# Attention and gated FFN on one core: q laid out as 128 partitions by 4 with 64 queries apart

## The chip, the core and the metric

The program runs on one core of a Trainium2 chip. The metric is the device time of one execution in microseconds (us), the median of several. Engines are called PE (TensorE, matmuls; PEld is its weight load), DVE (VectorE), ACT (ScalarE), POOL (GpSimd) and SP (SyncE, which here only issues DMAs). SP and ACT issue hardware DMAs, POOL issues software DMAs; all run on the same 16 DMA engines.

## The reference

For 8 batches and 8 heads, q, k and v are 1152 x 64 in fp32. Neighbouring pairs of q rows are averaged (so 576 queries), then softmax attention with scale 1/8, then the heads are laid side by side (x is 4608 x 512), and a feed-forward part without a nonlinearity follows:

```python
q_pool = q.reshape(B, H, S // 2, 2, D).mean(axis=3)
scores = scale * np.matmul(q_pool, k.transpose(0, 1, 3, 2))
attn = np.exp(scores - max); attn = attn / (sum + 1e-09)
x = matmul(attn, v).transpose(0, 2, 1, 3).reshape(B * S, H * D)   # 4608 x 512
a = x @ w1; b = x @ w2                                           # 512 -> 1024
out = ((a * b) @ w3) @ w_out                                     # 1024 -> 1024 -> 512
```

## The kernel before

**Pairs.** Two heads of one batch make a pair; there are 32 pairs (8 batches by 4). For each pair the kernel loads k, q and v into `kst`, `qst` and `vst` (lines 178, 180, 186; 576 KB each), casts k to fp16 (`kpair`, line 192), adds neighbouring q rows into fp16 (`qs`, line 198; on DVE for pair 0, on POOL for the others) and casts v with an extra column for the row sum (`vaug`, line 205). `qst` has 96 partitions (QP) with 6 pooled queries each (QC), for each head 3072 contiguous bytes a partition. Query 6p + c stands in partition p, block c, so after a transpose the columns of `qpT` hold the queries in the order c, p: a permutation that the output store undoes.

**Transposes.** Scores need d on the partitions. For pairs 0 to 7 PE transposes (`transp_pe`, lines 221 and 224: six blocks of q, nine of k, into one PSUM tile, then three DVE copies at lines 225 to 227). For pairs 8 to 31 SP issues DMA transposes (`transp`, lines 210 and 212), one pair ahead of their use.

**Scores and values.** `scores` (line 240) walks the 9 x 576 columns of a pair in groups of 512 into PSUM tiles `psc` (three of them), and ACT writes the exponentials into an SBUF ring (line 245). `av_pair` (line 259) multiplies 128 queries at a time ("unit": five per pair, the fifth overlaps the fourth and only its last 64 rows are new) with `vaug` into `avb`, and `av_norm` (lines 276, 284) divides by the row sum.

**xT.** The FFN needs x transposed: `xT` has 4 slots of 128 feature rows (one per pair of a batch) by 2880 columns, a ring of five batches of 576 columns. Units of pairs 0 to 19 get there by a PE transpose (line 289) and a DVE copy (line 296), those of pairs 20 to 31 by two DMA transposes per pair on SP (lines 269 and 271: 4 blocks of 128 and one of 64 columns).

**FFN.** w3 @ w_out is folded into `T16` early (lines 315, 324). The 4608 columns of `xT` are worked off in 9 chunks of 512: 16 groups of 4 matmuls (line 345, two per hidden block, evacuated at 365 or 367 and multiplied at 370), then 4 output tiles of 128 rows (line 377), scaled into `osb` (three buffers; lines 383, 386, 387, 390) and stored (line 355). The very last tile of chunk 8 is computed in two halves (lines 399, 401) and stored from ACT's queue. Because a 128-row tile crosses the 96-row blocks of the query order, `store` cuts each tile into two DMAs.

**Order.** It is written out by the Python code, not by a scheduler: in each visit three groups of scores, one or two units of `av_pair`, and one or two groups of the FFN queue ("fill"). A chunk joins the queue when the unit that completes it is done (`done_at`); chunks that depend on DMA-transposed x wait ten units more (`held`). After the last scores come the rest of the units and then the rest of the queue, chunks 6 to 8, with ACT helping to evacuate (`tail`).

**Queues.** Loads of pairs 0 and 1: SP and ACT. Loads of pairs 2 to 9: POOL, with w3, w_out, w1 and w2 between them. Loads from pair 10 on (v from pair 8 on) and all DMA transposes: SP, in program order. Output stores before the tail: POOL; in the tail: SP. At the end all engines read a flag (line 583), and SP waits for every DMA to land.

Of the kernel before, what the change touches and what calls it, by code (L numbers as in the profile page):

```python
# [8 lines left out]
FP32 = mybir.dt.float32  # L9
FP16 = mybir.dt.float16  # L10
AF = mybir.ActivationFunctionType
ALU = mybir.AluOpType
# [11 lines left out]
def _general(tc, q, k, v, out, w1sb, w2sb, T16):  # L24
# [8 lines left out]
    NF = dff // 128  # L33
    QP = 96
    QC = Sq // QP
    SCALE = 0.5 * float(D) ** -0.5
# [3 lines left out]
    with tc.tile_pool(name="gen", bufs=1) as sb, \  # L40
# [3 lines left out]
        for h in range(H):  # L44
# [5 lines left out]
            nc.sync.dma_start(out=vst, in_=vf[bass.ds(ih, 1)].rearrange("o (c p) d -> p (o c) d", p=128))  # L50
            qst = sb.tile([QP, QC, 2, D], FP32, tag="g_qst")
            nc.sync.dma_start(out=qst, in_=qf[bass.ds(ih, 1)].rearrange("o (c p t) d -> p (o c) t d", p=QP, t=2))
            kh = sb.tile([128, NJ, 128], FP16, tag="g_kh")
            qh = sb.tile([QP, QC, 128], FP16, tag="g_qh")
            vh = sb.tile([128, NJ, D], FP16, tag="g_vh")
# [6 lines left out]
            nc.sync.dma_start(out=kT, in_=kh.rearrange("p c d -> p (c d)"), transpose=True)  # L62
            qT = sb.tile([128, QC, QP], FP16, tag="g_qT")
            nc.sync.dma_start(out=qT, in_=qh.rearrange("p c d -> p (c d)"), transpose=True)
            kTf = kT.rearrange("p c i -> p (c i)")
            pav = ps.tile([128, 1024], FP32, tag="g_pav")
            for c in range(QC):
                pss = ps.tile([128, S // W, 512], FP32, tag="g_pss")
# [24 lines left out]
        for ft in range(NF):  # L93
            for n0 in (0, NH):
# [8 lines left out]
                nc.vector.tensor_tensor(out=gT[:, ft, n0:n0 + NH], in0=pb[:, 0:NH], in1=asb, op=ALU.mult)  # L103
        for c in range(QC):
            po = ps.tile([128, 512], FP32, tag="g_po")
# [9 lines left out]
def kernel(  # L115
# [11 lines left out]
    nc = tc.nc  # L127

    B, H, S, D = q.shape
    Sq = S // 2  # L130
# [5 lines left out]
    HP = H // 2  # L136
# [2 lines left out]
    G = 512  # L139
    NS = NP * FLAT // G  # L140
    RING = 24 * Sq
    QP = 96
    QC = Sq // QP
    E1 = D + 1
    SCALE = 0.5 * float(D) ** -0.5
    SCL = 16.0
    TO = [0, 128, 256, 384, Sq - 128]
    NT5 = len(TO)
# [6 lines left out]
    att = fast.enter_context(tc.tile_pool(name="att", bufs=2))  # L155
# [3 lines left out]
    ident16 = const.tile([128, 128], FP16)  # L159
# [13 lines left out]
    kq, vs, pairs = {}, {}, {}  # L173

    def load_kq(p, k_eng, q_eng):
        b, h0 = p // HP, 2 * (p % HP)
        kst = att.tile([128, 2, NJ * D], FP32, tag="kst")
        k_eng.dma_start(out=kst, in_=k[b, h0:h0 + 2].rearrange("u (p c) d -> p u (c d)", p=128))
        qst = att.tile([QP, 2, QC * 2 * D], FP32, tag="qst")
        q_eng.dma_start(out=qst, in_=q[b, h0:h0 + 2].rearrange("u (p c) d -> p u (c d)", p=QP))  # L180
        kq[p] = (kst, qst)

    def load_v(p, eng):
        b, h0 = p // HP, 2 * (p % HP)
# [2 lines left out]
        vs[p] = vst  # L187

    def cast_kq(p):
        kst, qst = kq.pop(p)  # L190
        kpair = att.tile([128, NJ, 2, D], FP16, tag="kpair")
        nc.gpsimd.tensor_copy(out=kpair.rearrange("p c u d -> p u c d"),  # L192
                              in_=kst.rearrange("p u (c d) -> p u c d", d=D))
        qs = att.tile([QP, QC, 2, D], FP16, tag="qs")
        qv = qst.rearrange("p u (c t d) -> p u c t d", t=2, d=D)
        eng = nc.vector if p == 0 else nc.gpsimd
        for u in range(2):
            eng.tensor_tensor(out=qs[:, :, u, :], in0=qv[:, u, :, 0, :], in1=qv[:, u, :, 1, :], op=ALU.add)  # L198
        pairs[p] = [kpair, qs]

    def cast_v(p):
        va = vaugs[p % NVA]
# [2 lines left out]
        nc.gpsimd.tensor_copy(out=va[:, :, :, 0:D], in_=vs.pop(p).rearrange("p u (c d) -> p u c d", d=D))  # L205

    def transp(p):
        kpair, qs = pairs[p]
        kT2 = att.tile([128, NJ, 128], FP16, tag="kT2", bufs=3)
        nc.sync.dma_start(out=kT2, in_=kpair.rearrange("p c u d -> p (c u d)"), transpose=True)  # L210
        qpT = att.tile([128, QC, QP], FP16, tag="qpT", bufs=3)
        nc.sync.dma_start(out=qpT, in_=qs.rearrange("p c u d -> p (c u d)"), transpose=True)
        pairs[p] = (kT2, qpT.rearrange("p c i -> p (c i)"))

    def transp_pe(p):
        kpair, qs = pairs[p]
        kT2 = att.tile([128, NJ, 128], FP16, tag="kT2", bufs=3)
        qpT = att.tile([128, QC, QP], FP16, tag="qpT", bufs=3)
        pt = ps.tile([128, 2, 512], FP32, tag="psc", bufs=3, name="ptk").rearrange("p b c -> p (b c)").bitcast(FP16)
        for c in range(QC):  # L220
            nc.tensor.transpose(pt[:, c * QP:c * QP + QP], qs[:, c].rearrange("p u d -> p (u d)"), ident16[0:QP, 0:QP])  # L221
        cols = [Sq + c * 128 if c < 3 else 1024 + (c - 3) * 128 for c in range(NJ)]
        for c in range(NJ):
            nc.tensor.transpose(pt[:, cols[c]:cols[c] + 128], kpair[:, c].rearrange("p u d -> p (u d)"), ident16)  # L224
        nc.vector.tensor_copy(out=qpT.rearrange("p c i -> p (c i)"), in_=pt[:, 0:Sq])  # L225
        nc.vector.tensor_copy(out=kT2[:, 0:3].rearrange("p c i -> p (c i)"), in_=pt[:, Sq:Sq + 384])
        nc.vector.tensor_copy(out=kT2[:, 3:NJ].rearrange("p c i -> p (c i)"), in_=pt[:, 1024:1024 + (NJ - 3) * 128])  # L227
        pairs[p] = (kT2, qpT.rearrange("p c i -> p (c i)"))


    def scores(s):
# [16 lines left out]
    XR = 5 * Sq  # L248
    xT = att.tile([128, NC, XR], FP16, tag="xT", bufs=1)
    xbts = {}  # L250

    def av_pair(i):
        p, t = i // NT5, i % NT5
        va = vaugs[p % NVA]
        o = (i % 3) * 2 * E1
        for jt in range(NJ):
            c0 = ((p * NJ + jt) * Sq) % RING + TO[t]
            for u in range(2):
                nc.tensor.matmul(avb[:, o + u * E1:o + u * E1 + E1], ring[:, u, c0:c0 + 128], va[:, u, jt, :],  # L259
                                 start=(jt == 0 and u == 0), stop=(jt == NJ - 1), skip_group_check=True)  # L260
# [3 lines left out]

    def x_dma(p):
        b, hp = p // HP, p % HP
        c0 = (b * Sq) % XR
        xb = xb5.pop(p)
        nc.sync.dma_start(out=xT[:, hp, c0:c0 + 512].rearrange("p (t i) -> p t i", i=128),
                          in_=xb[:, 0:4].rearrange("p t u d -> p (t u d)"), transpose=True)  # L270
        nc.sync.dma_start(out=xT[:, hp, c0 + 512:c0 + Sq],
                          in_=xb[Sq - 512:128, 4].rearrange("p u d -> p (u d)"), transpose=True)

    def av_norm(i):
        av = avb[:, (i % 3) * 2 * E1:(i % 3) * 2 * E1 + 2 * E1].rearrange("p (u e) -> p u e", e=E1)
# [15 lines left out]
    def x_copy(i):  # L291
        p, t = i // NT5, i % NT5
        b, hp = p // HP, p % HP
        r0 = 0 if t < NT5 - 1 else NT5 * 128 - Sq
        c0 = (b * Sq + TO[t] + r0) % XR
        nc.vector.tensor_copy(out=xT[:, hp, c0:c0 + 128 - r0], in_=xpt[:, r0:128])  # L296


# [35 lines left out]
    CH = 512  # L334
# [11 lines left out]
                                 start=(mc == 0 and d0 == 0), stop=(mc == NC - 1), skip_group_check=True)  # L346

    def store(eng, pos, osb):
        r = 0
        while r < 128:  # L350
            b, a = (pos + r) // Sq, (pos + r) % Sq
            cc, p0 = a // QP, a % QP
            n = min(QP - p0, 128 - r)
            dst = out[b * Sq:b * Sq + Sq, :].rearrange("(p c) n -> p c n", c=QC)[p0:p0 + n, cc, :]
            eng.dma_start(out=dst, in_=osb[r:r + n, :])  # L355
            r += n

    def moe_groups(c):
        gT = msb.tile([128, NF, CH], FP16, tag="g8", bufs=2, name="gT")
# [76 lines left out]
    def w_load(dst, src):  # L436
        nc.gpsimd.dma_start(out=dst, in_=src.rearrange("(c p) f -> p c f", p=128))

    load_kq(0, nc.sync, nc.scalar)
    load_v(0, nc.sync)  # L440
    load_kq(1, nc.scalar, nc.scalar)
    nc.gpsimd.memset(ident16, 0.0)
    nc.gpsimd.affine_select(
        out=ident16, in_=ident16, compare_op=ALU.not_equal, fill=1.0,
        base=0, channel_multiplier=1, pattern=[[-1, 128]],
    )
    cast_kq(0)
    w3_load(0)
    w_load(wosb, moe_w_out)
    cast_kq(1)  # L450
    load_kq(2, nc.gpsimd, nc.gpsimd)
    load_v(1, nc.gpsimd)
    cast_v(0)
# [20 lines left out]
    pair_end = [((p + 1) * FLAT - 1) // G // VS for p in range(NP)]  # L474
    done_at = {}
    for c in range(B * Sq // CH):
        b, r = ((c + 1) * CH - 1) // Sq, ((c + 1) * CH - 1) % Sq
        done_at.setdefault((b * HP + HP - 1) * NT5 + min(r // 128, NT5 - 1), []).append(c)

    avn, xn = [0], [0]  # L480
    ready, held = [], []
# [28 lines left out]
    while vis < NVIS or avn[0] < NU:  # L510
# [4 lines left out]
        if vis < NVIS:  # L515
            for s in range(vis * VS, vis * VS + VS):
                pn = (s * G + G - 1) // FLAT
                if pn != seen:
                    seen = pn
                    if pn == 0:  # L520
                        transp_pe(0)
                    if NPE <= pn + 1 < NP:
                        transp(pn + 1)
                    if pn + 2 < NP:
                        prepare(pn + 2)
                    elif pn + 2 == NP:
                        cast_v(NP - 1)
                scores(s)
        elif vis > NVIS:
            tail[0] = True  # L530
# [86 lines left out]
```

## Time and profile before

| | us |
|---|---|
| median of three runs | 430.56 (430.5 to 430.72) |
| the profiled execution's own time | 430.84 |
| its span, first to last instruction | 428.8 |
| PE busy | 408.0 |
| ACT busy | 326.7 |
| DVE busy | 205.5 |
| POOL busy | 178.7 |
| PE idle before its first instruction | 7.9 |

The page of the profile gives busy time per engine, the span in 40 slices, the DMA queues, the chain of work that ended last, and groups of instructions with their mean duration in ns and the idle time ahead of them. The granted TensorE clock was 0.998. The trace behind it also holds each DMA packet with its queue, size and duration, and each DMA's issue and landing.

### The profile page before, as it was taken

How to read it: one execution, taken by the hardware profiler on the slowest of the kernel's cores; microseconds unless marked ns; L12 is line 12 of the kernel's file. 1: busy time of each engine (PE TensorE's matmuls, PEld its weight loads, DVE VectorE, ACT ScalarE, POOL GpSimd, SP SyncE). 2: the span in 40 equal slices, each digit the busy share in tenths (PEclk: the TensorE clock that was granted, in tenths of full speed). 3: DMA queues.
4: the chain of work that ended last, by engine and by line, in shares of the span. 5: the costliest groups of instructions: out<-in, count | busy, mean ns of one | idle time of the engine just before them, and what ended most of it. 6: DMA issues, size and time to landing. Idle time of an engine off the chain costs nothing.

```text
span 428.8 us, 12736 instructions
## 1 busy us (share of the span) xinstructions
PE 408.0 (95%) x5317; PEld 251.2 (59%) x5317; DVE 205.5 (48%) x626; ACT 326.7 (76%) x359; POOL 178.7 (42%) x215
## 2 busy tenths in 40 slices
PE   1799999999999999999999999999999999999993
PEld 1376666666565656665666656665677856444442
DVE  1144564666356554655465635554445536534330
ACT  1889788889988988999889998999999980232221
POOL 3776755744675317630684218431861021000000
PEclk9999999999999999999999999999999999999999
DMA  8999999999999996999699949999795023030303
GB/s 254 250 262 264 251 232 229 264 230 239 276 296 289 256 216 205 278 232 270 178 252 280 307 100 240 254 252 240 216 205 108 15 64 69 10 99 0 99 1 105
DMA packets 79537, 84.59 MB, mean 197 GB/s; under 512 B 53489, under 2 KB 54513, under 8 KB 79473
## 3 DMA queue, kind: packets, MB, share of 16 engines
q1 hardware_dynamic: 70080, 56.57, 57.0%
q0 software_dynamic: 8544, 25.11, 23.7%
q10 hardware_dynamic: 848, 2.03, 1.7%
q8 instruction: 43, 0.70, 0.7%
q14 instruction: 22, 0.17, 0.1%
HBM read 67.11 MB, written 9.44 MB: 179 GB/s over the span
## 4 chain that ended last, share of the span: by engine, by line
PE 92%; DVE 3%; ACT 2%; DMA 2%; issue 0%; POOL 0%; ACTq 0%
PE avb L259 21%; PE psc L240 18%; PE mot L345 16%; PE mo L345 14%; PE mo L377 10%; PE mot L377 5%; PE mo L324 3%; ACT ring L245 2%; DMA kst<-in_k_dram 2%; PE avb L289 1%; PE ptk L224 1%; PE ptk L221 1%; DVE qpT L225 1%; PE mol L399 0%; PE mot L324 0%; DVE kT L227 0%
## 5 line engine op out<-in xcount | busy, mean ns | idle before, releaser
L245 ACT ACTIVATE ring<-psc 128x1024 f16<-128x1024 f32 x324 | 308.0, 1025 | 41.7 <-PE psc L240 38.7
L259 PEld LDWEIGHTS <-ring 128*128 128x128 f16 x2880 | 104.4, 98 | 36.5 <-issue 11.8
L259 PE MATMUL avb<-vaug,ring 128*128 128x65 f16 x2880 | 114.1, 193 | 2.1 <-DVE xT L296 1.4
L240 PE MATMUL psc<-qpT,kT 64*128 64x512 f16 (+7 forms) x1152 | 94.9, 291 | 2.8 <-ACT ring L245 1.8
L355 POOL DMA_DIRECT2D out_dram<-osb x48 | 25.1, 526 | 105.9 <-DVE rzall L276 105.8
L198 POOL TENSOR_TENSOR qs<-qst 96x384 f16<-96x384 f32 x62 | 60.5, 996 | 13.9 <-DMA qst<-in_q_dram 12.4
L240 PEld LDWEIGHTS <-kT 64*128 64x128 f16 x1152 | 45.5, 95 | 29.6 <-issue 6.1
L192 POOL CAST kpair<-kst 128x1152 f16<-128x1152 f32 x32 | 37.1, 1158 | 53.0 <-DMA kT<-kpair 22.5
L276 DVE RECIPROCAL rzall<-avb 128x2 f32<-128x2 f32 x160 | 26.6, 166 | 46.3 <-PE avb L289 30.8
L345 PEld LDWEIGHTS <-w2sb 128*128 128x128 f16 x320 | 28.6, 97 | 27.0 <-issue 2.8
L345 PEld LDWEIGHTS <-w1sb 128*128 128x128 f16 x320 | 28.4, 98 | 27.3 <-issue 3.4
L377 PEld LDWEIGHTS <-gT 128*128 128x128 f16 x280 | 25.5, 98 | 31.2 <-issue 4.0
L377 PE MATMUL mo<-T,gT 128*128 128x512 f16 x184 | 43.7, 380 | 0.0
L345 PE MATMUL mot<-xT,w2sb 128*128 128x512 f16 (+2 forms) x172 | 41.1, 364 | 0.0
L370 DVE TENSOR_TENSOR gT<-mot,asb 128x512 f16<-128x512 f32 x40 | 27.7, 692 | 24.2 <-PE mot L345 24.2
L205 POOL CAST vaug<-vst 128x1152 f16<-128x1152 f32 x32 | 36.6, 1145 | 6.1 <-DMA vst<-in_v_dram 6.0
L345 PE MATMUL mot<-xT,w1sb 128*128 128x512 f16 (+2 forms) x152 | 38.0, 373 | 0.0
L365 ACT COPY asb<-mot 128x512 f32<-128x512 f32 x21 | 12.3, 586 | 32.6 <-PE mot L345 32.6
L345 PE MATMUL mo<-xT,w1sb 128*128 128x512 f16 (+2 forms) x168 | 36.1, 344 | 0.0
L390 DVE TENSOR_SCALAR osb<-mo 128x512 f32<-128x512 f32 x23 | 15.9, 692 | 42.1 <-PE mo L377 42.1
L367 DVE COPY asb<-mo 128x512 f32<-128x512 f32 x35 | 24.2, 691 | 23.7 <-PE mo L345 23.7
L345 PE MATMUL mo<-xT,w2sb 128*128 128x512 f16 (+2 forms) x148 | 33.0, 351 | 0.0
(57 smaller groups left out, 266.8 us busy)
## 6 DMA issues: line engine op xcount, KB each, us to landing
vst<-in_v_dram SPq DMA_DIRECT2D x25, 576.0 KB, 6.2
kst<-in_k_dram SPq DMA_DIRECT2D x23, 576.0 KB, 6.9
qst<-in_q_dram SPq DMA_DIRECT2D x22, 576.0 KB, 8.1
kst<-in_k_dram POOLq DMA_DIRECT2D x8, 576.0 KB, 11.9
qst<-in_q_dram POOLq DMA_DIRECT2D x8, 576.0 KB, 13.6
vst<-in_v_dram POOLq DMA_DIRECT2D x7, 576.0 KB, 7.8
out_dram<-osb POOLq DMA_DIRECT2D x16, 192.0 KB, 3.4
w3c<-in_moe_w_dram POOLq DMA_DIRECT2D x4, 512.0 KB, 9.2
```

The lines of the kernel that those rows point to most:

```text
L192: nc.gpsimd.tensor_copy(out=kpair.rearrange("p c u d -> p u c d"), in_=kst.rearrange("p u (c d) -> p u c d", d=D))
L198: eng.tensor_tensor(out=qs[:, :, u, :], in0=qv[:, u, :, 0, :], in1=qv[:, u, :, 1, :], op=ALU.add)
L205: nc.gpsimd.tensor_copy(out=va[:, :, :, 0:D], in_=vs.pop(p).rearrange("p u (c d) -> p u c d", d=D))
L240: nc.tensor.matmul(psc[:, u, f - s * G:f - s * G + ln], kT2[u * 64:u * 64 + 64, jt, :], qpT[u * 64:u * 64 + 64, i0:i0 + ln], start=True, s ...
L245: nc.scalar.activation(out=ring[:, :, r0:r0 + G], in_=psc, func=AF.Exp, bias=0.0, scale=SCALE)
L259: nc.tensor.matmul(avb[:, o + u * E1:o + u * E1 + E1], ring[:, u, c0:c0 + 128], va[:, u, jt, :], start=(jt == 0 and u == 0), stop=(jt == N ...
L276: nc.vector.reciprocal(out=rzall[:, i, :], in_=av[:, :, D:E1].rearrange("p u o -> p (u o)"))
L345: nc.tensor.matmul(pw[:, d0:d0 + n], wt[:, mc, ft * 128:ft * 128 + 128], xT[:, mc, a:a + n], start=(mc == 0 and d0 == 0), stop=(mc == NC - ...
L355: eng.dma_start(out=dst, in_=osb[r:r + n, :])
L367: nc.vector.tensor_copy(out=asb, in_=pa)
L370: nc.vector.tensor_tensor(out=gT[:, ft, :], in0=pb, in1=asb, op=ALU.mult)
L377: nc.tensor.matmul(po, gT[:, ft, tt:tt + 128], T16[:, ft, :], start=(ft == 0), stop=(ft == NF - 1))
```

## The change

q of a head is cut in two: the first 512 pooled queries go to 128 partitions with 4 each (`qst`, 2048 contiguous bytes per partition and head), the last 64 to 64 partitions with one each (`qtl`, 512 bytes). Each pair has one more load, its sum is one instruction for both heads plus one for the 64 queries, and its transposes are four blocks of 128 and one of 64. The columns of `xT` are laid out by two batches: 512 of the even batch, its 64, the 64 of the odd batch, its 512. So each 128-row output tile is either 128 rows of one block (one DMA) or the two groups of 64 (two DMAs). `done_at` is worked out from the new positions.

The instruction streams stand as follows. PE has the same order up to the tail, with 5 q transposes in place of 6 in each of 8 pairs. In the tail the last two chunks change places: chunk 8 (the 512 of the last batch) comes before chunk 7 (which now holds the 64s of the last two batches), so the split last tile with its store on ACT's queue (line 399 before) stands in front of chunk 7, and the program ends with an ordinary tile of chunk 7, whose two 64-row stores are on SP. SP has 24 more transposes and 22 more loads and stores each tile of the tail with one DMA (two for the last); POOL has 8 more loads, and 27 store DMAs for 48; ACT has two more loads at the start.

```diff
     def load_kq(p, k_eng, q_eng):
...
-        qst = att.tile([QP, 2, QC * 2 * D], FP32, tag="qst")
-        q_eng.dma_start(out=qst, in_=q[b, h0:h0 + 2].rearrange("u (p c) d -> p u (c d)", p=QP))
+        qst = att.tile([128, 2, QM * 2 * D], FP32, tag="qst")
+        qtl = att.tile([QT, 2, 2 * D], FP32, tag="qtl")
+        q_eng.dma_start(out=qst, in_=q[b, h0:h0 + 2, 0:QM * 256].rearrange("u (p c) d -> p u (c d)", p=128))
+        q_eng.dma_start(out=qtl, in_=q[b, h0:h0 + 2, QM * 256:S].rearrange("u (p t) d -> p u (t d)", t=2))
...
     def cast_kq(p):
...
-        for u in range(2):
-            eng.tensor_tensor(out=qs[:, :, u, :], in0=qv[:, u, :, 0, :], in1=qv[:, u, :, 1, :], op=ALU.add)
+        eng.tensor_tensor(out=qs.rearrange("p c u d -> p u c d"), in0=qv[:, :, :, 0], in1=qv[:, :, :, 1], op=ALU.add)
+        eng.tensor_tensor(out=qt, in0=qtl[:, :, 0:D], in1=qtl[:, :, D:2 * D], op=ALU.add)
...
     def transp(p):
...
-        nc.sync.dma_start(out=qpT, in_=qs.rearrange("p c u d -> p (c u d)"), transpose=True)
+        nc.sync.dma_start(out=qpT[:, 0:QM * 128].rearrange("p (c i) -> p c i", i=128),
+                          in_=qs.rearrange("p c u d -> p (c u d)"), transpose=True)
+        nc.sync.dma_start(out=qpT[:, QM * 128:Sq], in_=qt.rearrange("p u d -> p (u d)"), transpose=True)
...
     def transp_pe(p):
...
-        for c in range(QC):
-            nc.tensor.transpose(pt[:, c * QP:c * QP + QP], qs[:, c].rearrange("p u d -> p (u d)"), ident16[0:QP, 0:QP])
+        for c in range(QM):
+            nc.tensor.transpose(pt[:, c * 128:c * 128 + 128], qs[:, c].rearrange("p u d -> p (u d)"), ident16)
+        nc.tensor.transpose(pt[:, QM * 128:Sq], qt.rearrange("p u d -> p (u d)"), ident16[0:QT, 0:QT])
...
+    def xpos(b, t):
+        if b % 2 == 0:
+            return b * Sq + t * 128
+        return b * Sq + (QT + t * 128 if t < QM else 0)
...
     def store(eng, pos, osb):
-        r = 0
-        while r < 128:
...
-            eng.dma_start(out=dst, in_=osb[r:r + n, :])
-            r += n
+        b, r = pos // (2 * Sq) * 2, pos % (2 * Sq)
+        if r == QM * 128:
+            for u in range(2):
+                r0 = (b + u) * Sq + QM * 128
+                eng.dma_start(out=out[r0:r0 + QT, :], in_=osb[u * QT:u * QT + QT, :])
+            return
+        if r > QM * 128:
+            b, r = b + 1, r - QM * 128 - 2 * QT
+        eng.dma_start(out=out[b * Sq:b * Sq + QM * 128, :].rearrange("(p c) n -> p c n", c=QM)[:, r // 128, :], in_=osb)
...
-        b, r = ((c + 1) * CH - 1) // Sq, ((c + 1) * CH - 1) % Sq
-        done_at.setdefault((b * HP + HP - 1) * NT5 + min(r // 128, NT5 - 1), []).append(c)
+        last = max((b * HP + HP - 1) * NT5 + t for b in range(B) for t in range(NT5)
+                   if xpos(b, t) < (c + 1) * CH and xpos(b, t) + (128 if t < QM else QT) > c * CH)
+        done_at.setdefault(last, []).append(c)
```

`x_dma` and `x_copy` write the same blocks as before to the columns that `xpos` gives. QM is 4 and QT is 64.

## The prediction

> **What bounds the kernel now.** I read the page's busy times and its chain of work first, then the chain of the first 24 us, the timeline of the end, and the issues of DMAs.
>
> ```profile
> span 428.8 us, 12736 instructions
> ...
> PE 408.0 (95%) x5317; PEld 251.2 (59%) x5317; DVE 205.5 (48%) x626; ACT 326.7 (76%) x359; POOL 178.7 (42%) x215
> ...
> DMA  8999999999999996999699949999795023030303
> ...
> PE 92%; DVE 3%; ACT 2%; DMA 2%; issue 0%; POOL 0%; ACTq 0%
> ```
>
> PE is busy 408.0 of 428.8 us and is 92% of the chain. Of its 20.8 us of idle, 7.9 lie before its first instruction and 6.3 after its last; the middle has some 6.6, in pieces of under 1 us. So an edit pays if it takes instructions from PE or moves its beginning or its end. The DMA engines are as full as PE in the first two thirds, but PE waits there for no DMA.
>
> The chain of the beginning:
>
> ```profile
> 0.75 6.68 DMA kst<-in_k_dram
> 7.43 0.05 issue
> 7.48 1.37 POOL kpair L192
> 8.85 0.05 issue
> 8.90 1.16 PE ptk L224 x9
> ```
>
> The first k, not the first q, holds PE up: it lands at 7.43, POOL casts it, PE transposes it at 8.90. The first q is summed from 6.81 to 7.83.
>
> The end, from the timeline:
>
> ```profile
> 416.71 0.42 DVE L386 TENSOR_SCALAR osb<-mot 128x256 f32<-128x256 f32 x1 [0.97 <-PE mot L377]
> 417.17 0.38 ACT L387 ACTIVATE osb<-mot 128x256 f32<-128x256 f32 x1 [2.46 <-DVE osb L386]
> 417.57 0.79 SPq L355 DMA_DIRECT2D out_dram<-osb  x2
> ...
> 421.51 1.03 PE L399 MATMUL mol<-T,gT 128*128 128x256 f16 x8 [0.52 <-ACT osb L401]
> ...
> 422.58 0.38 ACT L401 ACTIVATE osb<-mol 128x256 f32<-128x256 f32 x1 [1.12 <-PE mol L399]
> 423.00 1.72 ACTq L355 DMA_DIRECT2D out_dram<-osb  x2
> ```
>
> In an ordinary tile of the tail ACT waits for DVE's half, so its store is issued 0.9 us after its last matmul; in the split last tile 0.45 after. By the trace the last store lands at 426.57, and SP's closing waits then take 2.25 us.
>
> **The change part by part.** The sum is made against the profiled execution's 430.84 us (2.0 around its span of 428.8); the median of the runs shown is 0.28 below it.
>
> *The first loads.* In the trace's packet records, each of the 16 DMA engines has 16 packets of the first k (2304 bytes) and 12 of the first q (3072 bytes), taken in turn. k's begin at 2.5 us. While both run a q packet takes about 160 ns and a k packet 125, and after q is done two streams of 2304-byte packets take 99 each: 12 x 285 + 4 x 197 = 4.2 us, and 0.6 to the landing, 7.3 against the 7.43 seen. With the change q has 16 packets of 2048 bytes. If they run as the k and v packets do, 99 x 2048/2304 = 88 ns: 16 x (99 + 88) = 3.0 us, landing at 6.1, 1.3 earlier. If they keep q's own rate (181 ns median for 3072 bytes, so 120): 16 x 219 = 3.5, landing at 6.6, 0.8 earlier. If each still takes 181: 4.5, 0.2 later.
>
> I take the k rate, since q's source is as contiguous as k's and what differs is the 96 partitions. The Trainium skill ("SBUF — State Buffer", Door 1: The DMA port swizzle) says that partitions 0 to 63 reach only the 8 even of 16 SBUF ports and 64 to 127 the odd ones; 96 partitions then load the even ports twice as heavily. The trace agrees in size (2304 bytes in 95 ns, 24 bytes a ns; 3072 in 181, 17 a ns). By that rule this term is -1.3, without it -0.8.
>
> But `qtl` now stands behind `qst` on ACT's queue, and PE takes its block before k's. 8 packets of 512 bytes per engine, between the 18 ns of 256-byte packets and the 98 of 1024-byte ones, alternate with v's 99: 0.9 to 1.6 us after `qst` (about 6.0), so 6.9 to 7.6. DVE's sums, 552 ns for 384 columns, become about 0.74 for 512 (done before that) and 0.2 to 0.5 for 128. PE can go on to k at 7.3 to 8.1, and k's own path gives 6.1 + 1.47 = 7.6. I take 7.8 for 8.90: **-1.1** (-1.3 to +0.2). ACT's two extra issues (0.47 each) end at 3.2, before its first exponential at 11.5.
>
> What PE gains at 8.9 stays: up to 18 us the chain is ACT's exponentials, then PE, and the DMA stream that feeds them starts at the same time and gets shorter.
>
> *The q transposes on PE.* Weight loads are 0.45 us for 6 of 96 rows and 0.88 for 9 of 128: 75 and 98 ns. 4 x 98 and one between 50 and 98 make 0.44 to 0.49 for 0.45. Eight times: -0.1 to +0.3; I take **+0.1**. DVE's copies keep their sizes.
>
> *Loads and sums on POOL.* The two sums of 996 ns become about 996 x 512/384 = 1328 and 332, so -0.33 us per pair. Each of 8 early pairs adds a `qtl` issue, about the 0.53 of a store's issue. 48 store issues become 27: -11 us. POOL is busy 42%; for pairs 1 to 7 its sums end 8 us or more ahead of PE's transposes (pair 7: 78.4 against 86.5). Zero, with that cover; without it +0.2 per early pair.
>
> *SP.* Per pair +0.34 (load) and +1.12 (the median issue of the 64-row transpose, line 271, the same shape); the 256-byte packets remain 576 for q. Behind them on SP stand v, k and q of later pairs. The trace has transposed k and q land 4 to 16 us before the pair's first score for pairs 11 to 31 (pair 10: 3.6). Pairs 8 and 9 have 1.3 and 2.5. There the DMA engines are the limit, and ten q loads ahead of pair 8 get shorter: 192 x 181/16 = 2.2 us become (256 x 88 + 128 x 45)/16 = 1.8, some 4 us in all. Zero; without that relief see the second rival.
>
> *The middle.* PE's order is the same. Chunk 1 now needs unit 39 instead of 38, in `xT` at 118.4, and starts at 121.4; chunk 3 needs 79 instead of 77, at 201.6 against 216.4. Zero; chunk 1 has 3 us of cover.
>
> *The tail.* The same matmuls in another order, so PE ends at about 422.6 again; the stall of 0.52 us in the split tile goes with it. The store is issued 0.93 + 0.04 after, at 423.55. Two 64-row stores on SP land 2.9 us after the first issue in three of four cases (420.8 to 423.7), 4.5 in the fourth, where an instruction fetch of 16 KB stood at 399.0 to 399.9. Such a fetch follows PE's end in this trace too (423.35 to 424.24), and ACT's second issue took 1.3 us in it. So 426.45 to 427.6 against 426.57: I take **+0.2** (-0.1 to +1.0). ACT issues chunk 8's last store in 0.4 to 1.3 us between two copies, of which PE notices nothing under 1 us, since it has three banks.
>
> Sum: -1.1 + 0.1 + 0.2 = **-0.8 us**: 430.0 for this execution, **429.8** for the median (-0.2%). 0.2% (0.86 us) is also about what a measurement of this kernel can tell from no change.
>
> **Rivals.**
>
> 1. *The beginning gains nothing.* q packets stay slow, or `qtl` comes late. For it: all this falls in 2 us in which several loads share the engines. Against it: the packet rates. 430.56 + 0.1 + 0.2 = 430.9.
>
> 2. *Slower: the transposes of pair 8 come late.*
>
> ```profile
> 86.23 0.34 SPq L180 DMA_DIRECT2D qst<-in_q_dram  x1
> 86.67 5.09 SPq L210 DMA_TRANSPOSE kT<-kpair  x1
> 91.81 2.41 SPq L212 DMA_TRANSPOSE qpT<-qs  x1
> 94.34 0.78 SPq L186 DMA_DIRECT2D vst<-in_v_dram  x1
> ```
>
> They land at 98.7 and 99.1, the first score is at 100.4 (counting line 240's matmuls by pair). With 0.53 (POOL's issue), 0.34 and 1.12 (SP's) and 0.3 for the third landing they come 2.3 later, and PE comes 1.1 earlier: a stall of 2.3 + 1.1 - 1.3 = 2.1, hence 429.8 + 2.1 = 431.9. It decides where the relief in the DMA stream is under 2.1 us at pair 8, half of the 4 worked out.
>
> 3. *Slower: the tail.* In the split tile, now in the middle, ACT writes the buffer that the store of three tiles before must have left. At that place DVE waited for such a store until 401.51; ACT would be ready at 400.4 and PE's second half waits behind ACT: +1.1, and with the late end +0.6 more: 431.5. Against it: that store was late by the fetch at 399.0, which comes 16 PE instructions later in the new program.
>
> 4. *More at the beginning* (k's path alone, and the end at 426.45): 429.2.
>
> 5. *`qtl` costs a whole DMA.* A 64 KB store of this size takes 2.0 us from issue to landing. If `qtl` comes 2.0 after `qst`, at 8.0, its sum ends at 8.3 and PE goes on to k at 8.4: a gain of 0.5 instead of 1.1, 430.4. Against it: the second of two stores on a queue lands 0.1 to 1.1 us after the first. The Trainium skill states this as a rule in the same page (The DMA setup-cost knee: some 2 us fixed per transfer); the stores bear out the 2.0, but not that it adds up along a queue.
>
> **How the numbers follow.** The forecast, with 4 as its good end, has 0.54; its own range, 429.2 to 430.4, has 429.70 (faster by 0.2%) near its middle, so 0.31 faster and 0.23 same. Rivals 1 and 5 have 0.10 and 0.06, same. Rival 2 has 0.15, slower; rival 3 has 0.10, slower at its full price and same at half, 0.07 and 0.03. The remaining 0.05 goes to collisions on POOL or SP that I did not find, slower. Faster 0.31, same 0.42, slower 0.27. The range runs from 429.0 to 431.9: it leaves out some 0.05 below and 0.10 above.
>
> **What would show it.** The first k landing at about 6.1 and PE's first k transpose at 7.6 to 8.0; hardware q packets of 2048 bytes at 85 to 90 ns; the first score of pair 8 with no wait before it; PE's last matmul 1 us earlier than 422.55, and the last landing 3.9 us after it or a little more. The prediction is wrong if k lands at 7 or later, if PE waits for `kT` or `qpT` near 100 us, or if the split tile's stall grows beyond 0.5.

## The result: slower, and where the time went

The changed kernel takes 433.9 us (median of six runs, 433.64 to 434.98) where the kernel before takes 430.64 beside it: a ratio of 1.0081 (95% interval 1.0068 to 1.0094). The forecast of 429.8 was wrong, and 433.9 is above its range. The profiled execution took 433.64 us with a span of 431.9.

The page of the changed kernel:

```profile
span 431.9 us, 12785 instructions
...
PE 408.9 (95%) x5309; PEld 250.9 (58%) x5309; DVE 206.2 (48%) x626; ACT 326.8 (76%) x359; POOL 165.2 (38%) x202
...
DMA  8999999789799997999999979999998022020102
...
PE 91%; DVE 4%; ACT 2%; DMA 1%; issue 0%; ACTq 0%; DVEq 0%
```

PE is busy 0.9 us longer, POOL 13.5 less, and the chain is still PE's. These averages don't show the loss; the two ends of the span do. PE's last matmul ends at 423.02 (422.55 before), so 0.47 of the span's 3.1 us are there, and 2.6 come after it: 8.9 us from PE's last matmul to the end of the span, where it was 6.25.

**The beginning.** The chain of the first 9 us:

```profile
0.75 5.37 DMA qst<-in_q_dram
6.12 0.02 issue
6.14 1.43 DVE qs L200
7.57 0.05 issue
7.62 0.61 PE ptk L226 x4
8.23 0.16 PE ptk L227
8.39 1.09 PE ptk L230 x9
```

The first k lands at 5.82 in the place of 7.43; the 2048-byte packets of q take 84 ns (median) where those of 3072 bytes took 181. But the chain no longer runs through k. It runs through q's sum on DVE, 1.43 us long. The two engines in the timeline, first after, then before:

```profile
5.87 1.14 POOL L194 CAST kpair<-kst 128x1152 f16<-128x1152 f32 x1 [4.55 <-DMA kst<-in_k_dram]
6.14 1.42 DVE L200 TENSOR_TENSOR qs<-qst 128x512 f16<-128x512 f32 x1 [6.14 <-DMA qst<-in_q_dram]
```

```profile
6.81 1.02 DVE L198 TENSOR_TENSOR qs<-qst 96x384 f16<-96x384 f32 x2 [6.81 <-DMA qst<-in_q_dram]
7.48 1.36 POOL L192 CAST kpair<-kst 128x1152 f16<-128x1152 f32 x1 [6.16 <-DMA kst<-in_k_dram]
```

Before, DVE started first, took 1.02 for two sums, and POOL's cast, begun 0.67 later, took 1.36. Now POOL starts first, its cast takes 1.14, and DVE's sum, begun 0.27 later, takes 1.42. PE's first k transpose comes at 8.32 by its own record, 0.58 earlier than before (8.90); 1.1 was expected.

**The transposes of pairs 1 to 7.** Pair 2 in the timeline (start, duration, engine, line), after and then before:

```profile
27.64 0.38 PE L226 MATMUL ptk<-ident,qs 128*128 128x128 f16 x4
27.95 0.20 PE L227 MATMUL ptk<-ident,qt 64*128 64x64 f16 x1
28.09 0.68 PE L230 MATMUL ptk<-ident,kpair 128*128 128x128 f16 x9
```

```profile
28.41 0.41 PE L221 MATMUL ptk<-ident,qs 96*128 96x96 f16 x6
28.66 0.67 PE L224 MATMUL ptk<-ident,kpair 128*128 128x128 f16 x9
```

From the first q transpose to the first k transpose it is 0.45 us where it was 0.25. The starts of the four 128-row transposes are 55 ns apart; the 64-row one starts 150 ns after the last of them, and the first k transpose 132 after that. Before, the six of 96 rows were 42 apart, and k followed 60 after the last. Pairs 2 to 7 each lose 0.20, and pair 1, still at the lower clock, 0.24.

By lining up the two traces matmul by matmul, PE's shift (after minus before) is -0.57 at the first k transpose, -0.34 after pair 1, -0.90 at 23 us, then -0.58, -0.38, -0.17, +0.03, +0.24 and +0.44 after pairs 2 to 7. From there it stays between +0.44 and +0.47 to the tail. The step at 23 us is the clock: full speed was granted at 24.27 us before and at 21.75 after. Of it 0.43 remain when pair 2 starts (-0.78). In the eleven profiles of this case that moment lies between 21.7 and 24.3 us, so that single profiles differ by some 0.4 to 0.6 us for it, and the medians decide.

**Pair 8** in SP's queue:

```profile
80.30 1.92 SPq L213 DMA_TRANSPOSE kT<-kpair  x1
82.28 1.25 SPq L215 DMA_TRANSPOSE qpT<-qs  x1
83.58 1.22 SPq L217 DMA_TRANSPOSE qpT<-qt  x1
84.92 0.51 SPq L188 DMA_DIRECT2D vst<-in_v_dram  x1
```

They are issued 6.4 us earlier than before and in 1.9 us where k's took 5.09; the last of the three lands at 87.8, 13 us ahead of the first score at 100.9.

**The end.** The last instructions in the timeline, and SP's wait after the branch that follows (time waited in total, times, longest), after and then before:

```profile
423.11 0.42 DVE L400 TENSOR_SCALAR osb<-mot 128x256 f32<-128x256 f32 x1 [1.36 <-PE mot L391]
423.57 0.38 ACT L401 ACTIVATE osb<-mot 128x256 f32<-128x256 f32 x1 [1.40 <-DVE osb L400]
423.98 1.63 SPq L366 DMA_DIRECT2D out_dram<-osb  x2
...
SPq L600 <- SPq L600: 2.7, 1, 2.7
```

```profile
SPq L585 <- SPq L585: 3.4, 1, 3.4
```

The trace's instruction records give SP's road. It issues the two stores until 425.61, reads the flag until 426.50, branches at 426.94, and executes its next instruction only at 429.66; the closing waits take 2.2 more. Both stores had landed by 427.48, 2.2 us before SP went on. Before, SP's last store was issued by 421.89, it branched at 423.22 and went on at 426.58. There the instruction behind the branch waits for the semaphore of the last store, from ACT, which landed at 426.57: so in the kernel before the landing did set the end, and the 3.4 in its row are in part this wait. In the ten other profiles that first wait is for a DMA that had landed before, and SP went on 2.5 to 3.2 us after its branch. An estimate from these: without the landing SP would have gone on at 425.7 to 426.4 in the kernel before. Its road was only 0.2 to 0.9 us shorter than the one over the landing, and the change made it 3.7 us longer up to the branch.

### The profile page after: what moved, and what is told of

Same layout as the page of the kernel before. It is cut to its first block, busy times and chain, and to the rows that moved or that the text cites. A ratio compares the mean times of both kernels' runs of the same rounds, so it can differ in the third digit from the quotient of the medians.

```text
span 431.9 us, 12785 instructions
## 1 busy us (share of the span) xinstructions
PE 408.9 (95%) x5309; PEld 250.9 (58%) x5309; DVE 206.2 (48%) x626; ACT 326.8 (76%) x359; POOL 165.2 (38%) x202
## 4 chain that ended last, share of the span: by engine, by line
PE 91%; DVE 4%; ACT 2%; DMA 1%; issue 0%; ACTq 0%; DVEq 0%
PE avb L271 21%; PE psc L246 18%; PE mot L358 15%; PE mo L358 14%; PE mo L391 10%; PE mot L391 5%; PE mo L337 3%; ACT ring L251 2%; PE ptk L230 1%; PE avb L302 1%; DMA qst<-in_q_dram 1%; PE ptk L226 1%; DVE w3T L331 1%; DVE qpT L231 1%; PE mol L413 0%; PE mot L337 0%
## 5 line engine op out<-in xcount | busy, mean ns | idle before, releaser
L370 POOL DMA_DIRECT2D out_dram<-osb x21 | 11.7, 556 | 97.1 <-DVE rzall L289 97.1
L200 POOL TENSOR_TENSOR qs<-qst 128x512 f16<-128x512 f32 x31 | 39.4, 1271 | 5.1 <-DMA qst<-in_q_dram 2.2
```

What stands on the lines that cost most here:

```text
L200: eng.tensor_tensor(out=qs.rearrange("p c u d -> p u c d"), in0=qv[:, :, :, 0], in1=qv[:, :, :, 1], op=ALU.add)
```

## The experiments

**The last store on ACT's queue.** The changed kernel, but its last tile's two stores are issued by ACT. Theory A: SP's own road after its last store sets the end. Theory B: the two 64-row stores and what surrounds them do.

```diff
-                    store(nc.sync, c * CH + tt, osb)
+                    end = (c + 2) * CH == B * Sq and tt + 128 == CH
+                    store(nc.scalar if end else nc.sync, c * CH + tt, osb)
```

> The changed kernel, with the two stores of the program's last tile issued from ACT's queue instead of SP's; nothing else. Theory A (the new end is SP's own road: in the changed kernel SP issues the last stores from 423.98 to 425.61, then reads the flag, branches at 426.9 and goes on only at 429.66, so every store issued on SP late pushes the end): SP is done with its stores at 422.5, branches by 424, and the end is set by the last landing or by SP's branch, 427 to 427.6, 2.0 to 2.6 earlier than 429.66. 433.9 becomes 431.3 to 431.9. Theory B (the end is the landing of the last tile's stores, late because they collide with an instruction fetch): the landing stays where it is and the time stays at 433.5 to 434.

Measured: 431.66 us, ratio to the kernel before 1.0024 (1.0012 to 1.0035), so 2.2 below the changed kernel. The end of its timeline:

```profile
424.17 0.38 ACT L401 ACTIVATE osb<-mot 128x256 f32<-128x256 f32 x1 [1.40 <-DVE osb L400]
424.58 1.62 ACTq L366 DMA_DIRECT2D out_dram<-osb  x2
```

The same two stores take the same 1.6 us to issue, and 6.3 us lie between PE's last matmul (423.62) and the end, where it was 8.9. SP now branches at 424.15, goes on at 426.66, and waits until 428.11 for the landing at 428.07. A holds, B falls: the landing is no earlier than in the changed kernel (427.48), and the end is 2.0 earlier.

**Chunk 7 ahead of chunk 8.** The changed kernel with the order of the last two chunks as before, so that the split tile and its store from ACT are last.

```diff
-    ready.extend(c for _, c in held)
+    ready.extend(sorted(c for _, c in held))
```

> The changed kernel, with chunk 7 put before chunk 8 again, so that the split tile with its store on ACT's queue is the last one, as it was before the change. Theory A: the end stands as before the change, 6.3 us after PE's last matmul: with PE's last matmul 0.5 later than before the change, 431.1 (430.8 to 431.4). Theory B says the same here. If the loss lies in the middle and not at the end, the time stays above 432.5.

Measured: 430.81, ratio 1.0002 (0.9987 to 1.0018). From PE's last matmul to the end it is 5.4 us, less than the 6.25 of the kernel before. About half of the 0.9 comes from the last tile, which is now one store (issued in 0.37 us) and not two (1.72), and lands 3.5 us after the last matmul and not 4.0. The other 0.4 lies behind the landing: 1.84 us to the end in place of 2.25. SP checks the DMAs' semaphores one after the other; the last store's is the first in this list in the kernel before and the sixth here, so that five checks are over when it lands. The order of the last two chunks is worth 3.1 us, nearly the whole slowdown of 3.3; the queue alone was 2.2 of it.

**The kernel before with its last stores on SP.** If A is right, this alone makes the kernel before slower.

```diff
-                store(nc.scalar, c * CH + tt, osb)
+                store(nc.sync, c * CH + tt, osb)
```

> The kernel before the change, with one word changed: the two stores of its last tile (32 and 96 rows) are issued from SP instead of ACT. Theory A: SP reads the flag and branches only after them, 3 us later than before: 433 to 434 against 430.6. Theory B (landing decides): the stores are issued at the same moment and land at the same time: 430.3 to 431.

Measured: 432.0, ratio 1.0037 (1.0024 to 1.0051).

```profile
420.65 3.37 SPq L355 DMA_DIRECT2D out_dram<-osb  x3
...
421.93 0.38 ACT L401 ACTIVATE osb<-mol 128x256 f32<-128x256 f32 x1 [1.12 <-PE mol L399]
...
SPq L585 <- SPq L585: 2.5, 1, 2.5
```

The direction is A's and the size is less than half of the 3 us expected: PE's last matmul to the end is 7.8 us. SP's last issue ended at 424.02, its branch at 425.05, it went on at 427.51, and the stores had landed by 425.85, 1.7 us before. So SP's road is the end here too, but three of its pieces are shorter than in the changed kernel: the first store is issued 0.45 after PE's last matmul (split tile) and not 0.96, the flag is read in 0.55 and not 0.84, and SP stands still for 2.5 after the branch and not 2.7.

**The 64 queries padded to 128 rows.** The changed kernel; PE transposes a 128-row tile whose upper 64 rows are zeros, and only the first 64 columns are used.

```diff
+        qt = att.tile([128, 2, D], FP16, tag="qt")
+        if p < NPE:
+            nc.gpsimd.memset(qt[QT:128], 0.0)
...
-        nc.tensor.transpose(pt[:, QM * 128:Sq], qt.rearrange("p u d -> p (u d)"), ident16[0:QT, 0:QT])
+        nc.tensor.transpose(pt[:, QM * 128:QM * 128 + 128], qt.rearrange("p u d -> p (u d)"), ident16)
```

> The changed kernel, but for pairs 0 to 7 the tile of the 64 queries has 128 partitions, the upper 64 set to zero by POOL, and PE transposes all 128 rows (columns 64 to 127 of the result are then overwritten by k's first block). The wait for the sum of the 64 queries stays. Theory C (a weight load of 64 rows between weight loads of 128 rows has to wait for the matmuls ahead, and the next load of 128 rows again: 150 and 132 ns in place of 55): from the first q transpose to the first k transpose of pairs 2 to 7 it takes 0.28 to 0.30 us instead of 0.447, 1.1 to 1.3 us in all eight pairs, 433.9 becomes 432.7. Theory D (the 0.2 us per pair is the wait for one more producer): the gaps stay at 0.447 and the time at 433.9.

Measured: 432.88, ratio 1.0048 (1.0030 to 1.0066), 1.0 below the changed kernel.

```profile
28.06 0.38 PE L228 MATMUL ptk<-ident,qs 128*128 128x128 f16 x4
28.28 0.22 PE L229 MATMUL ptk<-ident,qt 128*128 128x128 f16 x1
28.34 0.67 PE L232 MATMUL ptk<-ident,kpair 128*128 128x128 f16 x9
```

A transpose of twice the size makes the sequence shorter: 0.28 us to the first k transpose, all gaps 55 or 56 ns. So it is the 64 rows between 128-row tiles that cost 0.17 us a pair, not one more weight load. The kernel before shows the same price elsewhere, since scores work on 64 rows:

```profile
119.85 0.22 PE L289 MATMUL avb<-ident,xbt 128*128 128x128 f16 x1
120.00 0.83 PE L240 MATMUL psc<-qpT,kT 64*128 64x512 f16 x10
...
121.33 0.22 PE L289 MATMUL avb<-ident,xbt 128*128 128x128 f16 x1
121.38 1.03 PE L345 MATMUL mo<-xT,w1sb 128*128 128x512 f16 x4
```

At full clock 66 of its 128-row transposes of x are followed by a score matmul, which starts 150 ns later (median), and 27 by a 128-row matmul of the FFN, w3 or the output, which starts after 55. The Trainium skill has a rule for such a place ("TensorEngine Tiling (Array Packing)", Key Properties: a change of tiling mode drains TensorE). The 150 and 132 ns on the two sides of the 64-row tile, and their absence here, agree with it in kind; that it is a drain the traces don't show, and 96 rows followed by 128 had no such gap (60).

**Both repairs**, run twice.

> The changed kernel with both repairs at once: chunk 7 ahead of chunk 8 in the tail (the last store goes back to ACT), and the 64-query tile padded to 128 rows for the PE transposes. If the end and the 64-row transposes are two separate costs, they add up: 433.9 - 3.1 (chunk 7 first) - 1.0 (padding) = about 429.8, 0.8 to 0.9 below the kernel before (430.67 in the last comparison), which is the gain of the earlier start that the prediction summed. From the first q transpose to the first k transpose of pairs 2 to 7 it should show 0.28 us, as the padded kernel alone did (0.447 unpadded). If they are not separate (PE's earlier end is eaten by another wait at the end, as SP's or ACT's evacuation), the time stays at 430.5 to 431.0, that of chunk 7 first alone.

Measured: 429.87, ratio 0.9986 (0.9971 to 1.0002).

> The run with both repairs once more, as the measure for the two others on the same chip, and to settle whether it is below the kernel before: 429.87 against 430.91 (ratio 0.9986, 0.9971 to 1.0002) was on the edge. Theory of two separate costs: again a ratio of 0.998 to 0.999, 0.4 to 0.9 us below the kernel before. Rival, that only the clock's moment of switching made the difference: 0.9995 to 1.0005.

Measured: 429.95 against 431.07, ratio 0.9973 (0.9958 to 0.9989). The two costs add up (0.9 from 430.81 for chunk 7 first, 3.0 from 432.88 for the padded kernel). The second run puts the kernel with both repairs below the one before, by some 0.1 to 0.4%; the first alone doesn't. Its end, in the first of the two runs:

```profile
422.17 0.38 ACT L417 ACTIVATE osb<-mol 128x256 f32<-128x256 f32 x1 [1.12 <-PE mol L415]
422.58 0.37 ACTq L372 DMA_DIRECT2D out_dram<-osb  x1
```

PE's last matmul is at 422.13 and 422.50 in the two profiles (422.55 before), and the end 5.5 us after it in both (6.25). So 0.8 us of the gain lie behind PE's last matmul, 0.4 to the landing of the one whole store and 0.4 in SP's checks. The earlier beginning brings 0.0 to 0.4 in these profiles, less than the clock's moment shifts them. The time came out as the expectation summed it, and close to the prediction's 429.8, but its reason, the earlier start, holds for a third of it at most: that the numbers meet is luck.

**k's first cast on ACT.** Why does DVE's sum take 1.42 us?

```diff
-        nc.gpsimd.tensor_copy(out=kpair.rearrange("p c u d -> p u c d"),
-                              in_=kst.rearrange("p u (c d) -> p u c d", d=D))
+        cast = nc.scalar.copy if p == 0 else nc.gpsimd.tensor_copy
+        cast(out=kpair.rearrange("p c u d -> p u c d"), in_=kst.rearrange("p u (c d) -> p u c d", d=D))
```

> As the run with both repairs, with one more edit: pair 0's cast of k goes to ACT, which is idle then, in the place of POOL. It tests why DVE's first sum of q took 1.42 us for 512 columns where the one of 384 columns took 0.55 in the kernel before (0.74 by columns). Theory lock: DVE and POOL got in each other's way while POOL's cast ran beside the sum (5.87 to 7.01); without it the sum takes 0.70 to 0.80 us and ends near 6.9, PE's first q transpose starts at 7.0 to 7.1 in the place of 7.6, and the first k transpose is bound by the small q load (lands 7.58, sum 0.28, 64-row tile transposed by 8.0): 8.0 to 8.1 in the place of 8.3, so the time falls by 0.2 to 0.3 against the run with both repairs, less than that run can be told apart from. Theory shape: the sum takes 1.3 to 1.45 us for its own access pattern (4 blocks of 2 x 64 in a permuted order), wherever the cast runs; PE's first q transpose stays at 7.6 to 7.8 and the time is that of the run with both repairs.

Measured: 430.73, ratio 0.9994 (0.9983 to 1.0006). The beginning, from the timeline:

```profile
1.53 0.87 POOL L449 DMA_DIRECT2D w3c<-in_moe_w_dram  x1
...
5.91 1.15 ACT L198 CAST kpair<-kst 128x1152 f16<-128x1152 f32 x1 [0.36 <-DMA kst<-in_k_dram]
6.25 0.69 DVE L202 TENSOR_TENSOR qs<-qst 128x512 f16<-128x512 f32 x1 [6.25 <-DMA qst<-in_q_dram]
...
8.45 0.28 DVE L203 TENSOR_TENSOR qt<-qtl 64x128 f16<-64x128 f32 x1 [1.51 <-DMA qtl<-in_q_dram]
```

The same sum takes 0.69 us beside a cast on ACT, 1.42 beside one on POOL: so POOL's cast slows it, and its own shape does not. In the changed kernel both ran together for 0.87 us. The sum lost 0.73 by it and the cast nothing (1.14, where the mean of all is 1.15). The Trainium skill states it ("SBUF — State Buffer", SBUF: two separate sides): a DVE operation with two SBUF inputs and a POOL operation that reads SBUF hold a port pair one at a time, and the one that starts first keeps it for the whole instruction. The traces agree on who waits: in the kernel before DVE started first and POOL's cast was the long one (1.36). That the hold is for the whole instruction they don't quite show, as the sum of 0.69 ended 0.55 after the cast. The rest of the expectation failed. The free POOL issued its weight loads at 1.53 us, the small q load landed at 8.4, and PE's first k transpose came at 8.94, later than the 8.60 of the run with both repairs. The time is 0.9 above that run's, but the two intervals overlap.

**The weights held back.** On top of the run before: POOL casts pair 1's k before it issues the first weights.

```diff
     cast_kq(0)
+    cast_kq(1)
     w3_load(0)
     w_load(wosb, moe_w_out)
-    cast_kq(1)
```

> The run with k's cast on ACT, with POOL's first two weight loads put behind its cast of pair 1 (which waits for k, until about 10 us), so that they are again issued after the first q has landed. There the free POOL had issued them at 1.5 and 2.4 us, and the small q load landed at 8.4 in the place of 7.6. Theory: those weights took its share of the DMA engines; held back, it lands at 7.5 to 7.7, its sum ends by 7.95, the first k transpose starts at 8.0 to 8.1 (8.94 with the weights early, 8.32 in the changed kernel), and the time is 0.2 to 0.4 below that of the run with both repairs, repeated beside it: 429.4 to 429.7 if that gives 429.9. Rival: the small load is late for its place as the second on its queue, not for the weights; it still lands after 8.2 and the time stays at 430.3 to 430.9. Either way the first sum of q should take 0.7, as no cast of POOL runs beside it.

Measured: 435.41, ratio 1.0103 (1.0083 to 1.0122); a miss. From PE's timeline, and then a table by stretches of time (length; busy us of PE, PEld, DVE, ACT, POOL; granted clock; DMA share; GB/s):

```profile
32.37 1.04 PE L330 MATMUL mo<-ident,w3c 128*128 128x128 f16 x8 [2.53 <-DMA w3c<-in_moe_w_dram]
...
32.00:35.00 3.00, 2.63 (x33) 2.22 (x35) 1.12 (x4) 0.00 (x0) 2.90 (x6) 0.50 1.01 351
```

The small load lands 1.5 us behind the large one (7.98 against 6.45) where it was 2.2 with the weights early (8.43 against 6.23), so in these two profiles the weights cost it 0.7, and 1.5 remain without them. But PE's matmuls on w3 then wait 2.53 us for a weight, and in this pause, at 31.91, the granted clock falls to 0.50 for 3.4 us. Pair 2's transposes were 0.94 late before that. At pair 3 PE is 4.85 us behind the second run with both repairs, which leaves some 1.4 for the clock. The six executions bear this out: the one with a mean clock of 0.998 took 433.61, the others, at 0.988 to 0.995, 435.09 to 436.11.

**The small q load first**, and its sum first too, on top of the one before.

```diff
-        q_eng.dma_start(out=qst, ...)
         q_eng.dma_start(out=qtl, ...)
+        q_eng.dma_start(out=qst, ...)
```

> As the run before it, with the small q load issued ahead of the large one, and its sum ahead of the other: if the second place on the queue is what makes it land 1.5 us after the first, the small one now lands by 6.0 and the large one between 6.5 (its packets delayed by the small one's: 128 x 27 ns over 16 engines is 0.2 us, and a place in the queue 0.5) and 7.6 (it takes over the whole delay). First q transpose at 7.2 to 8.4, first k transpose 0.3 to 0.5 us after it, at 7.7 to 8.8; time 429.2 to 430.3. If the delay is one of the second place, the large load lands at 7.4 or later and nothing is gained over the run with the weights held; if it is the bytes ahead of it, the large one lands by 6.7 and the first k transpose starts at 7.8, the earliest of all.

Measured: 435.32, ratio 1.0099 (1.0078 to 1.0121), a miss too, with the same pause of PE (2.62 us).

```profile
5.84 0.28 DVE L202 TENSOR_TENSOR qt<-qtl 64x128 f16<-64x128 f32 x1 [5.84 <-DMA qtl<-in_q_dram]
8.57 0.69 DVE L203 TENSOR_TENSOR qs<-qst 128x512 f16<-128x512 f32 x1 [2.45 <-DMA qst<-in_q_dram]
```

Now the large load is second and lands 2.7 us after the small one, though only 128 packets of 27 ns, 0.2 us on 16 engines, stand before it. In both orders it is the second load on ACT's queue that is late. The packet records tell a part of the reason: the second's packets begin only when the first's are nearly or wholly through. In the changed kernel those of 2048 bytes run from 2.62 to 5.78 and those of 512 from 5.75 to 6.96; here those of 512 run from 4.09 to 5.01 and those of 2048 from 5.92 to 8.05. Why the small load's first packet comes at 4.09 here, and why 0.9 us pass before the large one's, is not settled.

## Why the prediction was wrong, point by point

- **The tail (+0.2, with -0.1 to +1.0) is the step that failed.** It measured +2.6. The prediction let the end hang on the landing of the last stores. For the kernel before that reading was right: SP went on 0.01 us after the landing for which it waited. The landing itself was forecast well, at 426.45 to 427.6, and came at 427.48. (By the prediction's own slow case, 4.5 us from the first issue to the landing, the bound should have been 428.05; it took 3.5.) What failed is that the end would still follow the landing. The prediction didn't cost the move of the stores to SP as work on SP's queue: issues until 425.61, flag 0.84, branch 0.4, 2.7 until SP goes on, 2.2 after the landing. The pieces stood in the trace of before, where SP branched at 423.22, 1.3 us after its last store, and DVE, whose wait there had been over since 418.9, stood still for 3.3 us after its own branch at 419.5. In every run whose last store was on SP the end lay 7.8 to 8.9 us after PE's last matmul; where it was on ACT, 5.4 to 6.3. The trace has two 8192-byte packets of an instruction queue between the branch and the next instruction (427.30 to 428.28 after). The Trainium skill ("Runtime: NRT & Kernel Launch", Instruction fetch mechanics) says that a taken branch to a page that is not held must fetch it first; the packets fit this, though they end 1.4 us before SP goes on and the trace doesn't name their engine.
- **The q transposes (+0.1, with -0.1 to +0.3) were mis-sized**: +1.4 for pairs 1 to 7, by the two gaps around the 64-row tile. The prediction added up weight loads (75 and 98 ns each), while equal neighbours start 42 and 55 ns apart, and took no price for a change of the row count, though the 150 ns stood in the trace of before. The padded run gave 1.0 back.
- **The first loads (-1.1, with -1.3 to +0.2): the mechanism was right, and half of it arrived.** Packets of 84 ns (88 predicted) and k at 5.82 (6.1) were right. The sum on DVE was costed at 0.74 from its columns, which is what it takes alone (0.69), but the earlier k puts POOL's cast ahead of it: 1.42. The first k transpose came 0.58 earlier. That the 96 partitions were what slowed the packets is not shown: they also got shorter, and no run changes one of the two alone. The small load landed at 7.58, 1.5 after the large one, inside the forecast's 0.9 to 1.6 and short of rival 5's 2.0. It held nothing up, because the large sum ended only at 7.56 and PE came to the 64-row tile at 8.16, 0.27 after its sum was done (7.89).
- **POOL, SP and the middle (0 each) were right.** POOL's sums measured 1271 and 450 ns (1328 and 332 predicted), and its busy time fell by 13.5 us. Rival 2 (pair 8 late) is refuted: 13 us of slack in the place of 1.3. The split tile in the middle brought no new wait for its buffer (PE waits 0.5 us for ACT there, as it did before), so rival 3's first half is refuted; its second half, the late end, was the right place with a quarter of the price.
- The chances had slower at 0.27, by cases in the middle and at the tail that ended at 431.9 at most. The true case was on that side of the list but not among them.

## What to carry to other kernels

The last DMAs of a program belong on the queue of an engine with the shortest road to the end after them: read for each engine what stands between its last issue and the end of the program, and work that road out anew when a change moves an issue to another engine. A landing that sets the end in one kernel need not set it in the next. A tile of another row count in a run of equal transposes can cost more than a padded one, so the shape of the neighbours is part of the price. An operand that arrives earlier may change which of two engines starts first, and with it who waits.

## What the runs showed of the hardware that was not expected

- At the end of the program SP stands still for 2.5 to 3.2 us between its branch and its next instruction where that waits for no landing (ten profiles), DVE for 2.8 to 3.3, ACT for 0.1 to 0.4.
- From the last landing to the end it takes 1.84 us where the last store's semaphore is the sixth that SP checks, 2.25 where it is the first.
- One 64-row transpose between 128-row ones costs about 0.17 us more than a 128-row one; a score matmul on 64 rows starts 150 ns after a 128-row transpose where a 128-row matmul starts after 55. Going from 96 to 128 rows costs nothing that shows (60).
- DVE's sum of two SBUF inputs takes 0.69 us with no POOL cast beside it and 1.42 with one.
- In a PE pause of 2.5 us (29.8 to 32.4) the granted clock fell to half, at 31.91, and stayed there for 3.4 us.
